# Infini-attention mix on one core: maxima turned to rows by VectorE, memory units split at head 16, first transfers in steps, later landings in the plan

## The chip, the cores and the metric

The kernel runs on one core of a Trainium2 chip. The metric is the device time of one execution in microseconds; lower is better. The core has a matrix engine (TensorE, called PE in the profile, with PEld for its weight loads), VectorE (DVE), ScalarE (ACT), GpSimd (POOL) and the queue that issues all transfers here (SyncE, SP). All five run their own instruction streams in program order and wait for each other by semaphores.

## The reference

There are two attention branches, A and B, over the same input `x` (2048 tokens, 640 features, 32 heads of 20). Each branch goes through the sequence in four segments of 512 tokens. In a segment it does causal softmax attention, reads a memory matrix that earlier segments have written, mixes both by a gate of the head, and then adds its own keys and values to the memory. A gate of the token mixes the two branches.

```python
for s in range(N):                       # four segments, in each of two branches
    logits = einsum("bhqd,bhkd->bhqk", qs, ks) * scale + mask
    a_dot = einsum("bhqk,bhkd->bhqd", softmax(logits), vs)
    num = einsum("bhld,bhde->bhle", phi(qs), M)
    den = einsum("bhld,bhd->bhl", phi(qs), z)[..., None] + 1e-6
    outs.append(g * num / den + (1.0 - g) * a_dot)
    M = M + einsum("bhld,bhle->bhde", phi(ks), vs)
    z = z + einsum("bhld->bhd", phi(ks))
out = gate * (A(x) @ A_wo) + (1 - gate) * (B(x) @ B_wo)
```

Products that need float32 precision are made of three matmuls: the high part of both operands, and each high part with the other's low part.

## The kernel before, in words

**Stages.** The work is eight windows, one for each segment and branch (segment 0 of A, segment 0 of B, segment 1 of A, and so on). A window has projections of q, k and v (`job_qk`, `job_v`: three terms of five 128-row pieces each), eight groups of four heads (a quad, numbered 0 to 63 over the run), memory reads (`mem_unit`), memory updates (`update_unit`) and an output projection (`job_o`).

**A quad** has two passes over its scores. The first (`s_unit`, L1236) computes scores with queries on the partitions, and VectorE takes the row maxima from them (L1223). The maxima, 32 numbers for each of 128 queries after a split into high and low parts (`m_unit`, L1247 on ACT and L1248 on POOL), must become rows, since they are fed back as extra rows of the operand `qst`: the second pass (`t_unit`, L1326) computes the scores with keys on the partitions, with the maximum already subtracted. ACT takes the exponential (L1318), POOL cuts the triangle (L1319), and `pv_unit` (L1346) multiplies by the values. First passes run two quads ahead of second passes, so that a quad's maxima are needed about one quad after they are made.

**Maxima to rows, before.** `mrow_unit` takes one of the eight PSUM banks and does two PE transposes (L1261, one on each half of the array). ACT then copies the bank to the tile `mr` (L1278), and two small transfers put it into `qst` (L1273).

**Two halves.** Most matmuls use 64 of the 128 rows of the array, so that two of them run side by side, one on each half (lane). The kernel fills both lanes from two lists. Projections and the other units fill the gaps between the units of the quads.

**The order is a plan.** The kernel holds a small planner that runs at build time. It keeps a clock and an assumed duration for each instruction, and it emits instructions in the order in which its own clock lets them start. `put` gives an engine an instruction, `dma` a transfer with an assumed time to land (`lat=` is added after the time that the bytes take). An engine's stream is fixed by that: where a transfer lands later than the plan assumed, the instruction that needs it stands in its engine's stream with others behind it. The table `RULES` gives, for each quad slot (the 66 steps of the main loop), the order of first-pass (S) and second-pass (T) units and seven numbers: how the slot's units are spread over its span, above which VectorE load late units are held back, the lag between the two lanes of one unit, the room kept, an earlier start and two waiting times.

**The start.** `warm_up` gives PE nine matmuls on zeros. The first two projections (q and k of the first 128 columns, `job_head`, L841) run on the whole array as the five pieces of `x` and the weights come in; nothing else can be done before. Seven more matmuls on zeros (`IDLE_STEPS`) stand among the first of them. `stage` asks for a weight piece: transfer to `wst` (three buffers), high part by ACT (L547), low part by VectorE (L549) for the first four pieces, by POOL after that. `want_x` does the same for a piece of `x` (L602, L592, L596).

**Memory reads.** `mem_unit` is called twice for each block of 128 tokens, with heads 0 to 18 and 19 to 31. The operand's channels (20 for each head) lie 128 to a tile, and each half of a tile (64 channels) is one float32 matmul, which the trace shows as two instructions. Heads that straddle a boundary of 64 channels are computed in both, with zeros where they don't belong.

Of the kernel before, what the change touches and what calls it, by code (L numbers as in the profile page):

```python
# [37 lines left out]
def r32(ap):  # L38
    return ap.bitcast(F32)
# [3 lines left out]
def tile_gated_mix_infini_attn(  # L43
# [314 lines left out]
    IDLE_STEPS = {3: 5, 4: 2}  # L358
# [136 lines left out]
    split = {}  # L495

    def stage(i):
        if i >= len(jobs) or i in staged:
            return
# [9 lines left out]
        if kind == "v":  # L509
# [6 lines left out]
            def piece(w, a, b, wh, wl, done):  # L516
# [14 lines left out]
                dma(0.53 * n, lambda: nc.sync.dma_start(out=w3, in_=src[m // 4][:, a:b, :]), landed, prio=need[i], lat=1.2)  # L531
# [4 lines left out]
        def got(w):  # L536
# [8 lines left out]
            def split_hi(pair):  # L545
                wh, wl = pair
                put("A", 0.625, lambda: nc.scalar.copy(wh, w3), lambda: put(  # L547
                    lo_eng, lo_cost,
                    lambda: lo.tensor_tensor(out=wl, in0=w3, in1=r32(wh), op=ALU.subtract), end, prio=3), prio=6)  # L549

                def end():
                    wst.give(w)
                    split[i] = pair
# [11 lines left out]
    def mix_weights(b):  # L565
# [16 lines left out]

        rows(0)

    xs = {}
    xuse = {}

    def want_x(s, k):
# [1224 lines left out]
```

## Time and profile before

| what | value |
|---|---|
| time, median of 3 runs | 1011.85 us (1010.74 to 1012.91) |
| profiled execution: its span, first to last instruction | 1010.0 us |
| the runs' median less that span | 1.85 us |
| PE busy | 998.5 us (99%) |
| VectorE busy | 751.3 us (74%) |
| ScalarE busy | 666.4 us (66%) |
| GpSimd busy | 602.4 us (60%) |
| transfers, share of 16 engines | 75.5% |

The profile gives no time of the profiled execution other than its span. A matmul's busy time holds its way through the array, in which the next one already streams, so that PE at 99% is not PE at its peak: what a matmul costs is seen from the start of one to the start of the next. Groups of instructions are named by line, engine and operation; `64*128 64x512` is a matmul on 64 rows of the array with 128 columns of weights and a 64x512 moving operand. `issue` as a releaser means that the engine waited for nothing that the profile shows.

### The profile page before, as it was taken

How to read it: one execution, taken by the hardware profiler on the slowest of the kernel's cores; microseconds unless marked ns; L12 is line 12 of the kernel's file. 1: busy time of each engine (PE TensorE's matmuls, PEld its weight loads, DVE VectorE, ACT ScalarE, POOL GpSimd, SP SyncE). 2: the span in 40 equal slices, each digit the busy share in tenths (PEclk: the TensorE clock that was granted, in tenths of full speed). 3: DMA queues.
4: the chain of work that ended last, by engine and by line, in shares of the span. 5: the costliest groups of instructions: out<-in, count | busy, mean ns of one | idle time of the engine just before them, and what ended most of it. 6: DMA issues, size and time to landing. Idle time of an engine off the chain costs nothing.

```text
span 1010.0 us, 30764 instructions
## 1 busy us (share of the span) xinstructions
PE 998.5 (99%) x11262; PEld 857.8 (85%) x11262; DVE 751.3 (74%) x2562; ACT 666.4 (66%) x1371; POOL 602.4 (60%) x1039
## 2 busy tenths in 40 slices
PE   9999999999999999999999999999999999999998
PEld 7998888978898888888889988888888897889776
DVE  4577677857897777786778857778676887789854
ACT  5476767767766677676676557766666575675682
POOL 4555657755575655666656466576675566556561
PEclk9999999999999999999999999999999999999999
DMA  7997879969796877896679677788666978658521
GB/s 241 282 313 238 284 249 317 296 197 280 241 307 211 268 224 213 255 274 204 180 227 289 196 230 229 215 273 277 200 198 201 304 235 248 201 190 269 155 89 63
DMA packets 146449, 236.42 MB, mean 234 GB/s; under 512 B 12950, under 2 KB 45883, under 8 KB 145979
## 3 DMA queue, kind: packets, MB, share of 16 engines
q1 hardware_dynamic: 146298, 234.46, 75.5%
q8 instruction: 89, 1.46, 0.6%
q14 instruction: 62, 0.50, 0.2%
HBM read 145.26 MB, written 94.65 MB: 238 GB/s over the span
## 4 chain that ended last, share of the span: by engine, by line
PE 91%; DMA 5%; DVE 2%; ACT 1%; issue 1%; SPq 0%; POOL 0%; DVEq 0%; ACTq 0%; POOLq 0%
PE bank L795 53%; PE bank L1346 14%; PE bank L1326 7%; PE bank L1236 7%; PE bank L905 3%; PE bank L987 3%; PE bank L947 2%; DMA wst<-in_a_wv_dram 1%; DMA row<-rowg 1%; PE bank L1261 1%; DMA qd<-row 1%; DMA row<-in_xT_dram 1%; DVE row L1411 1%; DMA dots<-row 1%; PE bank L1165 0%
## 5 line engine op out<-in xcount | busy, mean ns | idle before, releaser
L1223 DVE CUSTOM_DVE_ANT_0 bank<-bank,tri 128x256 f32<-128x256 f32 (+3 forms) x1024 | 474.5, 519 | 163.0 <-PE bank L1236 125.0
L795 PE MATMUL bank<-row,wh 64*128 64x512 f32 x2308 | 513.2, 402 | 0.0
L1318 ACT ACTIVATE p<-bank 128x512 f32<-128x512 f32 x548 | 301.5, 600 | 115.2 <-PE bank L1326 91.8
L795 PEld LDWEIGHTS bank<-row,wh 64*128 64x128 f32 x2308 | 329.1, 185 | 10.1 <-issue 0.2
L1319 POOL TENSOR_SCALAR_AFFINE_SELECT p<-p 128x256 f32<-128x256 f32 (+1 forms) x548 | 205.1, 382 | 200.6 <-ACT p L1318 187.1
L795 PE MATMUL bank<-row,wl 64*128 64x512 f32 x1154 | 312.5, 399 | 0.0
L549 POOL TENSOR_TENSOR wl<-wst,wh 128x640 fp32r<-128x640 f32 x115 | 180.1, 1569 | 72.7 <-ACT wh L547 69.5
L795 PE MATMUL bank<-wvh,row 64*128 64x320 f32 (+1 forms) x1280 | 191.0, 313 | 0.0
L795 PEld LDWEIGHTS bank<-row,wl 64*128 64x128 f32 x1154 | 182.9, 185 | 3.8
L1236 PE MATMUL bank<-kst,qst 60*128 60x384 f32 (+3 forms) x1024 | 177.1, 317 | 3.5 <-ACT mr L1278 2.0
L1326 PE MATMUL bank<-qst,kst 62*128 62x128 f32 (+3 forms) x1024 | 175.9, 317 | 1.3 <-DVE mx L1223 1.3
L795 PEld LDWEIGHTS bank<-wvh,row 64*128 64x128 f32 x1280 | 160.0, 185 | 2.1 <-issue 0.4
L1223 DVE DVE_READ_ACCUMULATOR2_ANT mx<- 128x1 f32 x1024 | 143.8, 140 | 0.0
L1346 PE MATMUL bank<-p,vst 128*32 128x384 f32 (+3 forms) x1836 | 141.4, 423 | 0.0
L1236 PEld LDWEIGHTS bank<-kst,qst 60*128 60x128 f32 x1024 | 132.6, 186 | 9.5 <-ACT mr L1278 2.8
L1326 PEld LDWEIGHTS bank<-qst,kst 62*128 62x128 f32 x1024 | 130.7, 186 | 6.8 <-DVE mx L1223 2.4
L1346 PEld LDWEIGHTS bank<-p,vst 128*32 128x32 f32 x1836 | 57.4, 110 | 80.9 <-issue 58.2
L795 PE MATMUL bank<-wvl,row 64*128 64x320 f32 (+1 forms) x640 | 109.1, 312 | 0.0
L547 ACT CAST wh<-wst 128x640 fp32r<-128x640 f32 x119 | 86.7, 740 | 25.1 <-PE bank L795 17.7
L795 PEld LDWEIGHTS bank<-wvl,row 64*128 64x128 f32 x640 | 87.0, 186 | 0.4 <-issue 0.2
L1376 ACT COPY row<-bank 128x512 f32<-128x512 f32 x58 | 34.2, 590 | 69.8 <-PE bank L1346 64.9
L524 POOL TENSOR_TENSOR wvl<-wst,wvh 128x640 fp32r<-128x640 f32 (+1 forms) x48 | 60.1, 1258 | 31.9 <-ACT wvh L521 30.9
(121 smaller groups left out, 1223.4 us busy)
## 6 DMA issues: line engine op xcount, KB each, us to landing
qst<-qd SPq DMA_DIRECT2D x128, 240.0 KB
kst<-kd SPq DMA_DIRECT2D x128, 240.0 KB
qd<-row SPq DMA_DIRECT2D x40, 512.0 KB
kd<-row SPq DMA_DIRECT2D x40, 512.0 KB
dots<-row SPq DMA_DIRECT2D x56, 256.0 KB
wst<-wmix SPq DMA_DIRECT2D x35, 320.0 KB
row<-dots SPq DMA_DIRECT2D x42, 256.0 KB
qd<-row SPq DMA_DIRECT2D x40, 256.0 KB
```

The source lines that it names most:

```text
L524: put("G", 0.77 * n, lambda: nc.gpsimd.tensor_tensor(out=wl[:, a:b, :VN], in0=w3, in1=r32(wh[:, a:b, :VN]), op=ALU.subtract), end, prio=4)
L547: put("A", 0.625, lambda: nc.scalar.copy(wh, w3), lambda: put(lo_eng, lo_cost, lambda: lo.tensor_tensor(out=wl, in0=w3, in1=r32(wh), op=AL ...
L549: lambda: lo.tensor_tensor(out=wl, in0=w3, in1=r32(wh), op=ALU.subtract), end, prio=3), prio=6)
L795: return nc.tensor.matmul(bank_of, lhsT=w[ROWS[half]], rhs=x_[ROWS[half]], start=start, stop=stop)
L905: return nc.tensor.matmul(pm[:, a - h0:c - h0, :].rearrange("p h e -> p (h e)"), lhsT=r32(pqTs[t, m][ROWS[half], P * n:P * (n + 1)]), rhs= ...
L1223: put("D", w / 960.0 + 0.105, lambda: nc.vector.tensor_tensor_reduce(out=sc[:, off:off + w], in0=sc[:, off:off + w], in1=tri[:, L - w:], s ...
L1236: lane_ops[half].append((mm(w), lambda pair=pair, qb=qb, off=off, w=w, r=r, sc=sc: nc.tensor.matmul(sc[:, off:off + w], lhsT=q[r, pair, P ...
L1318: put("A", 0.483, lambda: nc.scalar.activation(pt, sc, AF.Exp, scale=SCALE), lambda: (bank.give(sc), put("G", 0.15 + 0.105 * len(todo), la ...
L1319: "G", 0.15 + 0.105 * len(todo), lambda: nc.gpsimd.affine_select(out=blocks, in_=blocks, pattern=[[0, len(todo)], [1, P]], base=0, channel ...
L1326: lane_ops[half].append((mm(w), lambda pair=pair, kb=kb, off=off, w=w, r=r, sc=sc: nc.tensor.matmul(sc[:, off:off + w], lhsT=k[r, pair, P ...
L1346: nc.tensor.matmul(po[32 * j:32 * j + 32, P * kb:], lhsT=vst[t % 2][:, kb, h * E1:h * E1 + 32], rhs=pts[i, n, f][0][:, off:off + w], start ...
L1376: either(0.483, lambda: nc.scalar.copy(r32(oT), po), 0.605, lambda: nc.vector.tensor_copy(r32(oT), po), end, 2)
```

## The change

1. The maxima are turned to rows by VectorE: `mrow_unit` is gone, with its two PE transposes, its bank and its ACT copy. In its place VectorE does four transposes of 32x32 (`turn_rows`), straight from `mt` to `mr`. The two small transfers stay.
2. Memory units are split at head 16 (channel 320, a multiple of 64) and not at head 19.
3. The first transfers are issued in steps: at first three pieces of `x` are asked for, not five; the other two and the third and later weight pieces are asked for when the first piece of `x` has been split. The head's matmuls are chosen one by one as their operands' high or low parts are there, and the seven matmuls on zeros among them are gone.
4. The plan counts some transfers as landing later: v weights by 1.4 us (`lat` 1.2 to 2.6), `x` of later segments by 1.8 us, the two operands of the reciprocals by 1.0 us.
5. `RULES` has a new line for each slot.

```diff
@@ RULES
-        1: "STSTSTSTST 1.010 1.43 0.30 8 0.0 1.47 0.77",
+        1: "TTSTTSSTSS 1.01 2.38 0.3 8 0 1.6 1",
...
@@ warm_up
     WARM = 9
-    IDLE_STEPS = {3: 5, 4: 2}
@@ stage
-        if i >= len(jobs) or i in staged:
+        if i >= len(jobs) or i in staged or i >= len(HEAD0) and not x_begun:
             return
...
-                dma(0.53 * n, lambda: nc.sync.dma_start(out=w3, in_=src[m // 4][:, a:b, :]), landed, prio=need[i], lat=1.2)
+                dma(0.53 * n, lambda: nc.sync.dma_start(out=w3, in_=src[m // 4][:, a:b, :]), landed, prio=need[i], lat=2.6)
@@ want_x
             def end():
-                big.give(st)
                 xs[s, k] = (hi, lo)
+                if s:
+                    big.give(st)
+                    return
+                x_first.give(st, *([x_first_rows[-1]] if k == 0 else []))
+                if k == 0:
+                    x_begun.append(1)
+                    for i in range(len(HEAD0), 9):
+                        stage(i)
+                if k == KT - 1:
+                    big.give(*x_first_rows)
...
-                out=r32(st), in_=xT[P * k:P * (k + 1), L * s:L * (s + 1)]), landed, ..., lat=1.2 if s else 1.1)
+                out=r32(st), in_=xT[P * k:P * (k + 1), L * s:L * (s + 1)]), landed, ..., lat=3.0 if s else 1.1)
@@ job_head
-            for w, x_ in ((wh, xh), (wl, xh), (wh, xl)):
-                whole(STEP, lambda: nc.tensor.matmul(
-                    pps[i], lhsT=w[:, k, :], rhs=x_, start=(n[i] == 0), stop=(n[i] == 3 * KT - 1)))
-                n[i] += 1
-
-                for _ in range(IDLE_STEPS.get(sum(n.values()), 0)):
-                    idle_step()
-                yield STEP
+            w, o = split_hi_[i][j == 1], x_hi[0, k][j == 2]
+            whole(STEP, lambda: nc.tensor.matmul(
+                pps[i], lhsT=w[:, k, :], rhs=o, start=(n[i] == 0), stop=(n[i] == 3 * KT - 1)))
+            n[i] += 1
+            yield STEP
@@ mem_unit
-        h0, h1 = ((0, 19), (19, 32))[h]
+        h0, h1 = ((0, 16), (16, 32))[h]
@@ m_ready, mrow_unit
-        later(0, 0.2, lambda: True, lambda: mrow_unit(i))
+        mr_store.want(1, lambda mr: put("D", 0.4, lambda: turn_rows(i, mr), lambda: send_rows(i, mr), prio=1), prio=0)
+
+    def turn_rows(i, mr):
+        mt = mts.pop(i).rearrange("p f c n -> p (f c n)")
+        for j in range(NB):
+            nc.vector.transpose(r32(mr[:, 32 * j:32 * j + 32]), r32(mt[32 * j:32 * j + 32, :]))
...
-        b = bank.free.pop(0)
-        ops = [[(TURN, lambda a, z, r=r: nc.tensor.transpose(b[:32, r], mtf[r], ident[r, r]))] for r in ROWS]
...
-            put("A", 0.15, lambda: nc.scalar.copy(mr, b[:32, :P]), send, prio=1)
@@ reciprocals
-            out=r32(d), in_=lanes_of(t)[:, DH:DH + 1, :].to_broadcast([H, 4, L])), landed, prio=-1, lat=1.2)
+            out=r32(d), in_=lanes_of(t)[:, DH:DH + 1, :].to_broadcast([H, 4, L])), landed, prio=-1, lat=2.2)
...
@@ start of the program
+    big.want((F32,) * 4, lambda *rows: (x_first_rows.extend(rows), x_first.give(*rows[:3])))
     for k in range(KT):
         if k < len(HEAD0):
             stage(k)
         want_x(0, k)
-    for i in range(len(HEAD0), 9):
-        stage(i)
```

**Three places in the streams.** The first is SyncE's stream at the very start (weights to `wst`, pieces of `x` to `row`). Before:

```order
L558 DMA wst_142<-in_a_wq_dram 128x640
L602 DMA row_9_191<-in_xT_dram 128x512
L558 DMA wst_143<-in_a_wk_dram 128x640
L602 DMA row_16_194<-in_xT_dram 128x512
L602 DMA row_21_197<-in_xT_dram 128x512
L602 DMA row_26_200<-in_xT_dram 128x512
L602 DMA row_31_203<-in_xT_dram 128x512
L558 DMA wst_144<-in_a_wq_dram 128x640
L558 DMA wst_142<-in_a_wk_dram 128x640
```

and now:

```order
L566 DMA wst_142<-in_a_wq_dram 128x640
L622 DMA row_4_188<-in_xT_dram 128x512
L566 DMA wst_143<-in_a_wk_dram 128x640
L622 DMA row_5_189<-in_xT_dram 128x512
L622 DMA row_6_190<-in_xT_dram 128x512
L1746 DMA beta_199<-in_a_beta_dram 128x32
L1746 DMA beta_200<-in_b_beta_dram 128x32
L622 DMA row_4_188<-in_xT_dram 128x512
L622 DMA row_7_191<-in_xT_dram 128x512
L566 DMA wst_144<-in_a_wq_dram 128x640
```

The fourth piece of `x` goes into the buffer of the first (`row_4`), so that it and all behind it on SyncE wait until that piece has been split. The second place is PE's stream of the head (`wh`, `wl` weights; `row` the parts of `x`; `bank_134` q, `bank_135` k). Before:

```order
L349 MATMUL bank_141<-qst_80 128x512 x9
L841 MATMUL bank_134<-row_7_189,wh_145 128x512
L841 MATMUL bank_134<-row_7_189,wl_146 128x512
L841 MATMUL bank_134<-row_8_190,wh_145 128x512
L349 MATMUL bank_141<-qst_80 128x512 x5
L841 MATMUL bank_135<-row_7_189,wh_147 128x512
L349 MATMUL bank_141<-qst_80 128x512 x2
L841 MATMUL bank_135<-row_7_189,wl_148 128x512
L841 MATMUL bank_135<-row_8_190,wh_147 128x512
L841 MATMUL bank_134<-row_14_192,wh_145 128x512
```

and now:

```order
L356 MATMUL bank_141<-qst_80 128x512 x9
L868 MATMUL bank_134<-row_13_193,wh_145 128x512
L868 MATMUL bank_134<-row_13_193,wl_146 128x512
L868 MATMUL bank_134<-row_14_194,wh_145 128x512
L868 MATMUL bank_135<-row_13_193,wh_147 128x512
L868 MATMUL bank_135<-row_14_194,wh_147 128x512
L868 MATMUL bank_134<-row_20_195,wh_145 128x512
L868 MATMUL bank_135<-row_13_193,wl_148 128x512
```

The seven matmuls on zeros are gone, and the products with low parts stand behind those whose operands are there earlier. The third place is where maxima become rows. Before, on ACT, at the first v weights of the third window (`wvh` the high part of v weights, `mr` the rows, `p` exponentials):

```order
L1318 ACTIVATE p_4116_3592<-bank_138 128x512
L1318 ACTIVATE p_4117_3593<-bank_137 128x512
L521 CAST wvh<-wst_143 128x2x320
L1278 CAST mr_161<-bank_136 32x128
L1318 ACTIVATE p_4158_3623<-bank_135 128x512
L1318 ACTIVATE p_4157_3622<-bank_138 128x512
L521 CAST wvh<-wst_144 128x2x320
```

and now, on VectorE, at the same quad (`mx` the maxima of a first pass):

```order
L1247 ISA bank_139,mx_3436<-bank_139,tri 128x512
L1247 ISA mx_3436 128x1
L1283 STREAM_TRANSPOSE mr_161<-mt_3445 32x32 x4
L784 TENSOR_TENSOR row_3961_3464<-bank_136,row_3960_3463 128x512
L767 TENSOR_SCALAR bank_136<-bank_136 128x512
L768 TENSOR_TENSOR row_3962_3465<-bank_136,row_3962_3465 128x512
L1247 ISA bank_141,mx_3436<-bank_141,tri 128x384
```

The copy of the rows has left ACT, where it stood behind a cast of v weights, and the four transposes stand between two evacuations on VectorE. Counted over the streams, PE loses the 128 transposes of L1261 and 24 matmuls of `mem_unit` (264 to 240), VectorE gains 256 transposes, and ACT loses 64 copies.

More of the change, by code (lines that the diff above doesn't have):

```diff
@@ L546, in split_hi, with low @@
                 wh, wl = pair
-                put("A", 0.625, lambda: nc.scalar.copy(wh, w3), lambda: put(
-                    lo_eng, lo_cost,
-                    lambda: lo.tensor_tensor(out=wl, in0=w3, in1=r32(wh), op=ALU.subtract), end, prio=3), prio=6)
+                def low():
+                    split_hi_[i] = pair
+                    put(lo_eng, lo_cost, lambda: lo.tensor_tensor(out=wl, in0=w3, in1=r32(wh), op=ALU.subtract), end, prio=3)
+                put("A", 0.625, lambda: nc.scalar.copy(wh, w3), low, prio=6)
                 def end():
@@ L825, in job_head, with there @@
     def job_head():
-        todo = [(k, i) for k in range(KT) for i in range(len(HEAD0))]
+        todo = [(k, i, j) for k in range(KT) for i in range(len(HEAD0)) for j in range(3)]
         pps, n = {}, {}
+        def there(x):
+            k, i, j = x
+            return i in (split if j == 1 else split_hi_) and (0, k) in (xs if j == 2 else x_hi)
         while todo:
-            ready_ = [x for x in todo if x[1] in split and (0, x[0]) in xs]
-            if not ready_:
+            x = next((x for x in todo if there(x)), None)
+            if x is None:
                 blocked[0] = "head"
@@ L1253, in m_ready, with send_rows, sent @@
         m_done.add(i)
-        later(0, 0.2, lambda: True, lambda: mrow_unit(i))
-    def mrow_unit(i):
-        t, u, q, k = quad(i)
-        mt = mts.pop(i)
-        b = bank.free.pop(0)
-        mtf = r32(mt.rearrange("p f c n -> p (f c n)"))
-        ops = [[(TURN, lambda a, z, r=r: nc.tensor.transpose(b[:32, r], mtf[r], ident[r, r]))] for r in ROWS]
-        def got(mr):
-            def sent():
-                mr_done.add(i)
-                mr_store.give(mr)
-            def send():
-                bank.give(b)
-                done = then_all(2, sent)
-                for half in range(2):
-                    r = 64 * half + 60
-                    dma(0.3, lambda half=half, r=r: nc.sync.dma_start(
-                        out=r32(q[r:r + 2, :, :].rearrange("p a (b n) -> p (a b) n", b=NB)),
-                        in_=r32(mr[16 * half:16 * half + 16, :]),
-                    ), done, prio=-2, some=True, issue=0.68)
-            put("A", 0.15, lambda: nc.scalar.copy(mr, b[:32, :P]), send, prio=1)
-        return split_unit(*ops, lambda: mr_store.want(1, got))
+        mr_store.want(1, lambda mr: put("D", 0.4, lambda: turn_rows(i, mr), lambda: send_rows(i, mr), prio=1), prio=0)
[3 more added lines that the diff above has]
+            nc.vector.transpose(r32(mr[:, 32 * j:32 * j + 32]), r32(mt[32 * j:32 * j + 32, :]))
+    def send_rows(i, mr):
+        t, u, q, k = quad(i)
+        def sent():
+            mr_done.add(i)
+            mr_store.give(mr)
+        done = then_all(2, sent)
+        for half in range(2):
+            r = 64 * half + 60
+            dma(0.3, lambda half=half, r=r: nc.sync.dma_start(
+                out=r32(q[r:r + 2, :, :].rearrange("p a (b n) -> p (a b) n", b=NB)),
+                in_=r32(mr[16 * half:16 * half + 16, :]),
+            ), done, prio=-2, some=True, issue=0.68)
     def p_room():
@@ L1423, in reciprocals @@
         dma(0.8, lambda: nc.sync.dma_start(
-            out=r32(d), in_=lanes_of(t)[:, DH:DH + 1, :].to_broadcast([H, 4, L])), landed, prio=-1, lat=1.2)
+            out=r32(d), in_=lanes_of(t)[:, DH:DH + 1, :].to_broadcast([H, 4, L])), landed, prio=-1, lat=2.2)
         dma(0.8, lambda: nc.sync.dma_start(
-            out=r32(g), in_=rowg[t // 2][NB * b:NB * b + NB, :].rearrange("n p -> (n p)")[None, :].to_broadcast([P, L])), landed, prio=-1, lat=1.2)
+            out=r32(g), in_=rowg[t // 2][NB * b:NB * b + NB, :].rearrange("n p -> (n p)")[None, :].to_broadcast([P, L])), landed, prio=-1, lat=2.2)
     waiting = {}
```

21 lines of the change are left out of this document (13 added, 8 removed), and 123 rows, old and new, of the table RULES.

## The prediction

> **What bounds the kernel now.** I read the page first: the span, PE's share, then the chain that ended last, with its shares by line.
>
> ```profile
> span 1010.0 us, 30764 instructions
> PE 998.5 (99%) x11262; PEld 857.8 (85%) x11262; DVE 751.3 (74%) x2562; ACT 666.4 (66%) x1371; POOL 602.4 (60%) x1039
> PE 91%; DMA 5%; DVE 2%; ACT 1%; issue 1%; SPq 0%; POOL 0%; DVEq 0%; ACTq 0%; POOLq 0%
> by line: PE bank L795 52.8%; PE bank L1346 13.6%; PE bank L1326 7.2%; PE bank L1236 7.0%; PE bank L905 3.2%; PE bank L987 3.1%; PE bank L947 2.2%; DMA wst<-in_a_wv_dram 1.4%; DMA row<-rowg 0.9%; PE bank L1261 0.9%; DMA qd<-row 0.9%; issue 0
> ```
>
> PE is busy for 99% of the span and is 91% of the chain. Work that leaves PE's stream is therefore worth its step in that stream, and work on another engine is worth something only where PE waits for it. How often PE waits is said by the waits of PE alone:
>
> ```profile
> PE bank L1236 <- ACT mr L1278: 2.0, 2, 1.5
> PE bank L349 <- DVE qst L353: 1.5, 1, 1.5
> PE bank L1326 <- DVE mx L1223: 1.3, 1, 1.3
> PE bank L1236 <- ACT p L1318: 0.9, 2, 0.7
> PE bank L1236 <- ACT vst L1042: 0.6, 1, 0.6
> PE bank L947 <- DVE row L751: 0.4, 1, 0.4
> ```
>
> Without the start (L349) and the head (L947) that is 2.0 + 1.3 + 0.9 + 0.6 = 4.8 us in the whole run. The largest wait is for the ACT copy that the change removes. The timeline of PE and ACT around it shows why:
>
> ```profile
> 217.29 0.39 PE L1236 MATMUL bank<-kst,qst 60*128 60x512 f32 x1
> 219.13 0.50 PE L1236 MATMUL bank<-kst,qst 60*128 60x512 f32 x1 [1.45 <-ACT mr L1278]
> 218.20 0.72 ACT L521 CAST wvh<-wst 128x640 fp32r<-128x640 f32 x1 [2.16 <-DMA wst<-in_a_wv_dram]
> 218.83 0.25 ACT L1278 CAST mr<-bank 32x128 fp32r<-32x128 f32 x1
> ```
>
> ACT stands 2.16 us before a cast whose transfer has not landed; behind it stands the copy of the rows, which holds a bank, and PE waits 1.45 us for that bank.
>
> **The change part by part.** First, what leaves PE. From the groups of instructions, with shapes apart where it matters:
>
> ```profile
> L1261 PE MATMUL bank<-ident,mt 64*32 64x64 f32 x128 | 28.1, 219 | 0.2
> L1261 PEld LDWEIGHTS bank<-ident,mt 64*32 64x32 f32 x128 | 11.9, 93 | 9.1 <-issue 7.3 <-POOL row L1319 0.4 <-PE bank L795 0.3
> L947 PE MATMUL bank<-ident,row 64*128 64x64 f32 x304 | 31.5, 226 | 0.4 <-DVE row L751 0.4
> L947 PE MATMUL bank<-ident,O 64*128 64x64 f32 x240 | 19.5, 227 | 0.1
> L905 PE MATMUL bank<-mbd,row 64*128 64x84 f32 x432 | 47.8, 274 | 0.0
> L905 PE MATMUL bank<-mbd,row 64*128 64x63 f32 x48 | 8.5, 264 | 0.0
> L905 PE MATMUL bank<-mbd,row 64*128 64x21 f32 x48 | 8.1, 247 | 0.0
> ```
>
> The means of 219 to 274 ns hold the way through the array, so the steps come from the chain. The transposes of maxima have 0.9% of 1010.0 us, 9.1 us or 71 ns each for 128. The like transposes of L947 have 2.2%, 22.2 us for 304 + 240 = 544, 41 ns each; at that price 128 are 5.2 us. Weight loads before L1261 also stand 7.3 us idle, a part of which other half-array work covers. Bounds 0 (they fill holes beside the other half) and 9.1 us; I take **6.5 us**, nearer the like transposes.
>
> Memory units lose the pieces with 21 columns (head 19 alone), 48 instructions; 48 others grow from 63 to 84 columns. L905 has 3.2%, 32.3 us for 528, 61 ns each: 2.9 us go. Growing costs 274 - 264 = 10 ns for each of 48, 0.5 us, at most. **2.5 us**, bounds 0 and 2.9. On VectorE the two weighings change from 19 and 13 heads to 16 and 16, the same in sum.
>
> Second, what VectorE takes on: 256 transposes of 32x32, which this trace does not show. The nearest rows are small operations:
>
> ```profile
> L1223 DVE DVE_READ_ACCUMULATOR2_ANT mx<- 128x1 f32 x1024 | 143.8, 140 | 0.0
> L919 DVE SCALAR_TENSOR_TENSOR mw<-bank,gq 128x19 f32<-128x19 f32 x24 | 4.1, 171 | 1.6 <-PE bank L905 1.6
> L921 DVE RECIPROCAL mw<-mw 128x19 f32<-128x19 f32 x24 | 6.6, 276 | 0.8
> 275.00:400.00 125.00, 125.00 (x1443) 109.05 (x1440) 100.10 (x327) 82.42 (x168) 78.70 (x135) 1.00 0.80 245
> DVE bank L1223 <- PE bank L1236: 125.0, 141, 7.5
> ```
>
> Between 140 and 276 ns each, 256 make 35.8 to 70.7 us; I take 171 ns, 43.8 us, 0.68 us for a quad. VectorE then has 751.3 + 43.8 = 795 us. In its busiest stretch, the row 275:400 (VectorE is the third busy time), it has 100.1 of 125 us; eight quads more make 105.6, at the upper price 108.9. It stays under the bound, and its pauses before the maxima (125.0 us, 141 times, 0.89 us each) cover 0.68 us. I cost it at **0 us**; without that cover it is the second rival below. The ACT copies that go (64 of 249 ns, 15.9 us) are worth only the 2.0 us of PE's wait for them. The rows now pass from POOL to VectorE to the transfers, one engine less, and the second passes that wait for them come a quad later.
>
> Third, **the waits**. The change takes away the bank and the copy behind 2.0 of the 4.8 us. The transfers counted as later bear on that wait and on the 1.3 us one, which comes from the reciprocals:
>
> ```profile
> 418.12 0.75 DVE L1406 SCALAR_TENSOR_TENSOR row<-row,gcol,row 128x512 f32<-128x512 f32 x1 [2.62 <-DMA row<-rowg]
> 668.29 0.62 ACT L592 CAST row<-row 128x512 fp32r<-128x512 f32 x1 [3.12 <-DMA row<-in_xT_dram]
> ```
>
> VectorE stood 2.62 us before L1406 and ACT 3.12 us before a piece of `x`, each with other work behind. Counting 1.0 and 1.8 us more moves such instructions back, but by less than these waits. I take all of the 2.0, half of the other 2.8, and give back 0.4 for new waits of the new order: **3.0 us**. Bounds: 4.8 gained, and 4.8 lost if the new order has twice the waits. The table itself has no row; I price it at nothing beyond that, with 4 us either way, the size of all present waits.
>
> Fourth, **the head**. The timeline of PE, VectorE and ACT at the start:
>
> ```profile
> 1.52 4.21 PE L349 MATMUL bank<-qst 128*128 128x512 f32 x9 [1.52 <-DVE qst L353]
> 5.52 0.78 PE L841 MATMUL bank<-row,wh 128*128 128x512 f32 x1
> 6.69 1.31 PE L349 MATMUL bank<-qst 128*128 128x512 f32 x5
> 14.70 0.39 PE L841 MATMUL bank<-row,wh 128*128 128x512 f32 x1
> 15.02 0.27 PE L642 MATMUL bank<-ident,row 64*128 64x64 f32 x1
> 5.49 0.69 DVE L596 TENSOR_TENSOR row<-row,row 128x512 fp32r<-128x512 f32 x1
> 8.95 2.77 DVE L596 TENSOR_TENSOR row<-row,row 128x512 fp32r<-128x512 f32 x4 [1.58 <-ACT row L592]
> 3.83 0.73 ACT L547 CAST wh<-wst 128x640 fp32r<-128x640 f32 x1 [1.74 <-DMA wst<-in_a_wq_dram]
> 8.29 2.70 ACT L592 CAST row<-row 128x512 fp32r<-128x512 f32 x4 [1.78 <-DMA row<-in_xT_dram]
> 0.81 0.39 SPq L558 DMA_DIRECT2D wst<-in_a_wq_dram  x1
> ```
>
> The head's 30 matmuls lie between 5.52 and 15.02, 9.5 us. Next to each other they start about 0.235 us apart (five in 1.31 us, of which the last ends 0.39 after it starts: 0.92 / 4 = 0.23), 7.0 us for 30. So at most 2.5 us are to be had. Four pieces of `x` land together at 8.29, since four were asked for at once; now two are, and with half as much asked for they should land about 1 us earlier (an estimate). The last two are asked for after the first piece is split, at 5.49 + 0.69 = 6.2; a lone transfer here took 0.81 to 3.83, 3.0 us, so they land near 9.5 and 10, and with a cast of 0.7 and a subtraction of 0.7 the last is ready at 11.5, as before (8.95 + 2.77 = 11.7). PE then is bound by its own 24 matmuls from about 7.6: 13.2, and with small pauses 13.5. I take **1.5 us**; bounds 2.5 gained and 1.9 lost (the fourth rival).
>
> The first nine matmuls take 4.21 / 9 = 0.47 us each, and the five on zeros start 0.23 apart; the page of the Trainium skill "TensorE: Matmul & The Clock Gate", Part 1, says that the array starts at half clock, gets the full one after about 3.4 us of activity and loses it after an idle window as long. The trace agrees with the first half of that; by the second half the fillers can go as long as no pause lasts 3.4 us, and the sum stays as it is.
>
> **Sum**, against the profiled span: 1010.0 - 6.5 - 2.5 - 3.0 - 1.5 = 996.5 us. The runs' median lay 1011.85 - 1010.0 = 1.85 us over the span: **998.4 us**.
>
> **The rivals.** *PE's holes take it.* If transposes and short pieces lay where the other half was streaming, taking them away gives nothing, and 1010.0 - 3.0 - 1.5 + 1.85 = 1007.4 us. For it: PE's halves are filled from two lists. Against it: the chain gives L1261 71 ns each, more than its like. Chance 0.10.
>
> *VectorE holds PE.* The four transposes wait for POOL's subtraction L1248, and POOL's stream has long work:
>
> ```profile
> L549 POOL TENSOR_TENSOR wl<-wst,wh 128x640 fp32r<-128x640 f32 x115 | 180.1, 1569 | 72.7 <-ACT wh L547 69.5 <-DVE mx L1223 1.8 <-PE bank L1236 0.4
> DVE bank L1223 <- POOL mt L1248: 2.4, 1, 2.4
> ```
>
> If L1248 falls behind one of these, VectorE stands up to 1.57 us and then works 0.68, with the evacuations of the first passes behind it and PE short of banks. Of 2.25 us the mean pause covers 0.89; 1.36 us in one quad of four is 16 x 1.36 = 22 us: 998.4 + 22 = 1020 us. It decides once PE loses over 13.5 / 64 = 0.21 us in a quad. Against it: such meetings must come often, and now VectorE's maxima meet a late L1248 once, for 2.4 us. Chance 0.06.
>
> *New waits.* The new table and the later landings change where transfers and engines meet. Three times the 4.8 us, 14.4, instead of 1.8 that I leave, make 998.4 + 12.6 = 1011.0 us. For it: each of the present waits is an accident of one order. Against it: the counts go toward what the trace shows. Chance 0.09, of which 0.06 no change, 0.02 slower, 0.01 faster.
>
> *A slow head.* If PE without its fillers stays at the start's 0.47 us for eight matmuls more, 8 x 0.24 = 1.9 us are lost where 1.5 were gained: 998.4 + 1.5 + 1.9 = 1001.8 us. Against it stands that its pauses will be short. The clock gate above is this mechanism. Chance 0.05. That the change does less than it says, I leave out: the streams show transposes, pieces and transfers where it puts them.
>
> **How the numbers follow.** The forecast has 0.70, the rivals 0.10, 0.06, 0.09 and 0.05. About 2 us (0.2%) can be told from no change. Faster: 0.70 + 0.10 + 0.05 + 0.01 = 0.86; the same 0.06; slower 0.06 + 0.02 = 0.08. The best case is 9.1 + 2.9 + 4.8 + 2.5 = 19.3 us and 4 for the order: 988.6. For eight times in ten I cut that to 990 and take the holes rival in: 990 to 1008.
>
> **What would show it.** Right: no L1261; some 43 us more on VectorE in 256 transposes of about 0.17 us; 480 instructions in place of 528 for memory units; a head that ends near 13.5; PE's waits for engines under 4 us. Wrong: PE waiting for VectorE's maxima or for banks in many quads; transposes well over 0.3 us; PE's shares of all other lines grown by as much as the two lines lost.

## The result, and the profile after

| | median, us | lowest to highest | profiled span, us |
|---|---|---|---|
| before | 1011.45 (4 runs) | 1010.74 to 1012.91 | 1010.0 |
| changed | 998.3 (4 runs) | 997.94 to 999.33 | 996.5 |

The ratio of the changed kernel to the one before is 0.9878, with a 95% interval of 0.9859 to 0.9896: faster by 1.2%. Both the time and the span (996.5 us) came out where the prediction put them. The sections below show that several of its terms did not.

The head of the changed kernel's page has its span, the busy time of the engines, and the shares of the chain that ended last:

```profile
span 996.5 us, 30494 instructions
PE 989.4 (99%) x11079; PEld 843.6 (85%) x11079; DVE 794.0 (80%) x2818; ACT 654.1 (66%) x1305; POOL 603.4 (61%) x1041
PE 98%; DMA 1%; DVE 0%; SPq 0%; issue 0%; ACT 0%
```

PE still sets the time, and holds 98% of the chain, where it had 91%. The pieces of the chain that led over transfers (5%) are almost gone. The waits of PE alone, which had six rows before, have two:

```profile
PE bank L356 <- DVE qst L360: 1.5, 1, 1.5
PE bank L868 <- ACT row L602: 0.4, 2, 0.2
```

Both belong to the start. Of the 4.8 us of waits in the body none is left. The groups that replace L1261 and the split at head 19, and what VectorE waits for most (total, times, longest):

```profile
L1283 DVE STREAM_TRANSPOSE mr<-mt 32x32 f32<-32x32 f32 x256 | 51.0, 199 | 26.5 <-POOL mt L1272 23.9
L929 PE MATMUL bank<-mbd,row 64*128 64x84 f32 x480 | 46.5, 273 | 0.0
DVE bank L1247 <- PE bank L1260: 95.2, 126, 4.8
DVE mr L1283 <- POOL mt L1272: 23.9, 28, 2.4
```

A transpose takes 199 ns. The pauses before the maxima are 95.2 / 126 = 0.76 us each now, against 0.89. In 28 of the 64 quads VectorE stands before its transposes until POOL has the split maxima ready, 23.9 us in all. The timeline of VectorE shows the four transposes of one quad, and the table of stretches (PE, PEld, VectorE, ACT and POOL busy, with their counts) the stretch in which VectorE is now busiest and the one that the prediction spoke of:

```profile
103.90 0.84 DVE L1283 STREAM_TRANSPOSE mr<-mt 32x32 f32<-32x32 f32 x4
775.00:900.00 125.00, 125.00 (x1419) 106.95 (x1417) 105.30 (x362) 80.27 (x158) 74.97 (x129) 1.00 0.81 245
275.00:400.00 125.00, 124.94 (x1412) 106.50 (x1411) 103.45 (x362) 82.08 (x161) 79.16 (x135) 1.00 0.82 248
```

The four take 0.84 us, more than a pause of 0.76 us. The plan counts 0.4 us for them.

**Where the time went** can be read from the starts of the matmuls. The next table adds up, in each of the two traces, the time from the start of each PE instruction to the start of the next one, by the line of the first of the two. The last instruction counts with its own length. With 1.5 us ahead of the first and some 4 to 5 us behind the last, these steps make up the span.

| instructions | before: count, us | after: count, us | difference, us |
|---|---|---|---|
| projections (L795, L818) | 5400, 555.2 | 5400, 551.8 | -3.4 |
| transposes of maxima (L1261) | 128, 3.5 | none | -3.5 |
| first passes (L1236, L1260) | 1024, 89.0 | 1024, 86.8 | -2.2 |
| memory reads (L905, L929) | 528, 35.5 | 480, 33.3 | -2.3 |
| memory updates (L987, L1011) | 480, 36.9 | 480, 35.0 | -1.9 |
| matmuls on zeros (L349, L356) | 16, 5.6 | 9, 4.4 | -1.2 |
| the rest | 3686, 278.2 | 3686, 278.8 | +0.6 |

These are 14.0 us less in steps (before rounding), with 0.5 us more behind the last matmul. The table compares one execution with one. The traces of experiments 1 and 7 below have the order of the kernel before, and show how far executions of that order differ: 552.8 and 552.6 us for the projections, 87.6 and 87.7 us for the first passes, 36.0 and 35.6 for the memory reads, 36.6 and 38.6 for the updates. So most of the 3.4 us of the projections and of the 2.2 us of the first passes lies within that scatter, while memory reads and updates are shorter in the changed kernel than in all three. Such a table says where the steps are shorter, and not why.

### The profile page after: what moved, and what is told of

It is laid out like the page before. It is cut to its first block, busy times and chain, and to the rows that moved or that the text cites. A ratio compares the mean times of both kernels' runs of the same rounds, so it can differ in the third digit from the quotient of the medians.

```text
span 996.5 us, 30494 instructions
## 1 busy us (share of the span) xinstructions
PE 989.4 (99%) x11079; PEld 843.6 (85%) x11079; DVE 794.0 (80%) x2818; ACT 654.1 (66%) x1305; POOL 603.4 (61%) x1041
## 3 DMA queue, kind: packets, MB, share of 16 engines
q8 instruction: 87, 1.43, 0.6%
## 4 chain that ended last, share of the span: by engine, by line
PE 98%; DMA 1%; DVE 0%; SPq 0%; issue 0%; ACT 0%
PE bank L818 58%; PE bank L1364 15%; PE bank L1344 8%; PE bank L1260 8%; PE bank L1011 3%; PE bank L929 3%; PE bank L971 3%; PE bank L868 1%; DMA row<-in_xT_dram 1%; PE bank L1189 0%; DVE row L1174 0%; SPq L566 0%; ACT row L602 0%; PE bank L701 0%; DVE gate L643 0%
## 5 line engine op out<-in xcount | busy, mean ns | idle before, releaser
L1247 DVE CUSTOM_DVE_ANT_0 bank<-bank,tri 128x128 f32<-128x128 f32 (+3 forms) x1024 | 474.4, 520 | 104.0 <-PE bank L1260 95.2
L818 PE MATMUL bank<-row,wh 64*128 64x512 f32 x2308 | 497.2, 402 | 0.0
L1336 ACT ACTIVATE p<-bank 128x512 f32<-128x512 f32 x562 | 308.1, 603 | 122.1 <-PE bank L1344 104.7
L818 PEld LDWEIGHTS bank<-row,wh 64*128 64x128 f32 x2308 | 320.8, 185 | 13.0 <-issue 1.4
L818 PE MATMUL bank<-row,wl 64*128 64x512 f32 x1154 | 295.4, 398 | 0.0
L818 PE MATMUL bank<-wvh,row 64*128 64x320 f32 (+1 forms) x1280 | 183.3, 313 | 0.0
L818 PEld LDWEIGHTS bank<-row,wl 64*128 64x128 f32 x1154 | 175.5, 185 | 6.1 <-issue 1.2
L1344 PE MATMUL bank<-qst,kst 62*128 62x512 f32 (+3 forms) x1024 | 174.2, 321 | 0.0
L1260 PE MATMUL bank<-kst,qst 60*128 60x384 f32 (+3 forms) x1024 | 171.5, 316 | 0.1
L818 PEld LDWEIGHTS bank<-wvh,row 64*128 64x128 f32 x1280 | 153.1, 185 | 1.9 <-issue 0.8
L1260 PEld LDWEIGHTS bank<-kst,qst 60*128 60x128 f32 x1024 | 128.5, 186 | 7.9 <-issue 1.5
L818 PE MATMUL bank<-wvl,row 64*128 64x320 f32 (+1 forms) x640 | 107.8, 311 | 0.0
L818 PEld LDWEIGHTS bank<-wvl,row 64*128 64x128 f32 x640 | 87.1, 185 | 0.6 <-issue 0.2
L1283 DVE STREAM_TRANSPOSE mr<-mt 32x32 f32<-32x32 f32 x256 | 51.0, 199 | 26.5 <-POOL mt L1272 23.9
```

The source lines that it names most:

```text
L818: return nc.tensor.matmul(bank_of, lhsT=w[ROWS[half]], rhs=x_[ROWS[half]], start=start, stop=stop)
L1247: put("D", w / 960.0 + 0.105, lambda: nc.vector.tensor_tensor_reduce(out=sc[:, off:off + w], in0=sc[:, off:off + w], in1=tri[:, L - w:], s ...
L1260: lane_ops[half].append((mm(w), lambda pair=pair, qb=qb, off=off, w=w, r=r, sc=sc: nc.tensor.matmul(sc[:, off:off + w], lhsT=q[r, pair, P ...
L1283: nc.vector.transpose(r32(mr[:, 32 * j:32 * j + 32]), r32(mt[32 * j:32 * j + 32, :]))
L1336: put("A", 0.483, lambda: nc.scalar.activation(pt, sc, AF.Exp, scale=SCALE), lambda: (bank.give(sc), put("G", 0.15 + 0.105 * len(todo), la ...
L1344: lane_ops[half].append((mm(w), lambda pair=pair, kb=kb, off=off, w=w, r=r, sc=sc: nc.tensor.matmul(sc[:, off:off + w], lhsT=k[r, pair, P ...
```

## The experiments

The twelve kernels were measured in three groups of four, each group on another chip, and the kernel before was measured anew beside each group. Each time is set against the median before of its own group: 1011.13 us for doubled transposes on PE, maxima back on PE, doubled transposes on VectorE and the plan with 0.36 us; 1010.43 for half the transposes, the swap, the short pieces and the matmuls on zeros; 1010.3 for the other four. The changed kernel stood 13.15 us under its own.

**1. What do the PE transposes cost?** In the kernel before, each is issued twice, at the same place.

```diff
-        ops = [[(TURN, lambda a, z, r=r: nc.tensor.transpose(b[:32, r], mtf[r], ident[r, r]))] for r in ROWS]
+        ops = [[(TURN, lambda a, z, r=r: [nc.tensor.transpose(b[:32, r], mtf[r], ident[r, r]) for _ in range(2)][-1])] for r in ROWS]
```

> The kernel before, with each of its 128 PE transposes of maxima issued twice in place, so that 128 more stand in the same stream and nothing else moves; the output is the same. My step (they stand in PE's path at 41 to 71 ns each): 5.2 to 9.1 us more than before, about 6.5. The rival that they fill holes beside the other half of the array: within 1.5 us of before.

Measured: 1014.43 us (12 runs), ratio 1.0034, interval 1.002 to 1.0048. That is 3.3 us for 128 more transposes (2.0 to 4.9), 26 ns each (16 to 38). The steps in the table above say 3.5 / 128 = 27 ns. In this run's own trace the 256 transposes have 8.7 us of steps, 5.2 us more than the 128 before, 41 ns for each added one, so that 26 ns is no exact price. By the times this term is about 3.4 us and at most 4.9, not the 6.5 us that I took. Why the chain's share of 0.9% says more is not shown. What PE would gain without its transposes, and with nothing in their place, was not run. The Trainium skill, page "TensorE: Matmul & The Clock Gate", Part 1 (in the section on 56 ns and 53.3 ns), gives the time from start to start as the number of columns over 2.4 GHz, and 2.5 ns. For 64 columns that makes 29 ns, an estimate that lies within the 16 to 38 ns of the runs; it would have given 3.7 us.

**2. The maxima back on PE in the changed kernel**, everything else as changed: `mrow_unit`, bank and ACT copy instead of `turn_rows`.

```diff
-        mr_store.want(1, lambda mr: put("D", 0.4, lambda: turn_rows(i, mr), lambda: send_rows(i, mr), prio=1), prio=0)
+        later(0, 0.2, lambda: True, lambda: mrow_unit(i))
```

> The changed kernel with the maxima turned to rows by PE and copied by ACT, as before; all else as changed. The plan makes a new order of it. My steps: 6.5 us for the transposes and up to 2.0 us for a wait behind the copy, 1004.8 to 1006.8 us. If PE's holes take the transposes: under 1001 us. If VectorE's new work had cost PE time, this kernel would be faster than 998 us.

Measured: 1049.21 us, ratio 1.0371 (1.0348 to 1.0395). It does not price the step: with other durations the planner emits another order everywhere.

**3. Other orders.** How much the order alone weighs, three kernels show: the changed one with 0.36 us in place of 0.4 planned for the four transposes (the work is the same), the changed one with the table of before, and the kernel before with the new table.

```diff
-        mr_store.want(1, lambda mr: put("D", 0.4, lambda: turn_rows(i, mr), ...
+        mr_store.want(1, lambda mr: put("D", 0.36, lambda: turn_rows(i, mr), ...
```

> The changed kernel with the planned cost of the four transposes on VectorE 0.36 us in place of 0.4, which changes no work but makes the plan put instructions in another order. It measures what a new order alone is worth. If single steps can be told from orders: within 2 us of 998.3. If orders are worth as much as the steps: 3 to 8 us off, to the slower side, since the table was made for the other order.

> The changed kernel with the table of the kernel before. If the new table only adjusts (my 4 us either way): 994 to 1003 us. If a table fits one plan alone, as the run with another planned cost says (70 us slower by a plan cost of 0.36 for 0.4): 1030 to 1080 us.

> The kernel before with the new table. If the new table is better in itself: under 1011 us. If a table fits one plan alone: 1030 to 1080 us.

Measured: 1068.25 us, ratio 1.0562 (1.0539 to 1.0585); 1071.69 us, ratio 1.0604 (1.0582 to 1.0627); and 1061.95 us, ratio 1.0508 (1.0484 to 1.0531). A planned duration that differs by 0.04 us costs 70 us against the changed kernel; the table of the other kernel costs 73 us there and 52 us in the kernel before. So in these cases a table fits its own plan alone, and undoing one edit of the changed kernel measures the new order, not the edit. From here on I used only kernels that keep an order instruction for instruction.

Where does a bad order lose? In part by the clock. In the kernel with 0.36 us the mean granted clock is 0.984 of 1066.4 us, so about 1066.4 x 0.016 = 17 us of clock are missing (an estimate). Six stretches of 2 us of it, with the same columns as above (the one before the last two figures is the granted clock), and PE's timeline there:

```profile
178.00:180.00 2.00, 1.41 (x7) 0.67 (x5) 1.63 (x2) 1.97 (x5) 2.00 (x4) 1.00 0.64 219
180.00:182.00 2.00, 1.33 (x7) 0.86 (x7) 2.00 (x6) 2.00 (x5) 2.00 (x3) 0.96 0.07 24
182.00:184.00 2.00, 2.00 (x15) 2.00 (x14) 2.00 (x11) 1.81 (x4) 2.00 (x3) 0.50 0.00 0
184.00:186.00 2.00, 2.00 (x15) 2.00 (x14) 1.65 (x12) 0.00 (x0) 2.00 (x4) 0.50 0.14 38
186.00:188.00 2.00, 2.00 (x17) 2.00 (x15) 0.64 (x2) 0.00 (x0) 2.00 (x3) 0.50 0.42 126
188.00:190.00 2.00, 2.00 (x20) 1.90 (x19) 1.41 (x4) 0.82 (x2) 0.84 (x3) 0.84 0.00 0
178.68 0.43 PE L1260 MATMUL bank<-kst,qst 60*128 60x384 f32 x1 [0.19 <-ACT p L1336]
179.51 0.50 PE L1260 MATMUL bank<-kst,qst 60*128 60x384 f32 x3 [0.40 <-ACT vst L1066]
181.62 5.86 PE L1011 MATMUL bank<-vst,row 64*128 64x168 f32 x35 [0.64 <-ACT p L1336]
```

PE is busy for 1.41 and 1.33 of 2 us, with no pause over 0.64 us; then the clock stands at a half for 6.8 us (and in three later stretches, 34.1 us in all), and 35 memory updates take 5.86 us, 167 ns each, where the changed kernel's table above has 35.0 / 480 = 73 ns. The other 53 us or so of the loss lie spread over the stream; I did not trace them to single waits.

**4. Is VectorE's new work free?** The changed kernel's order is kept, and each transpose is issued twice, or only two of the four are issued, or none.

```diff
-        for j in range(NB):
+        for j in [j for j in range(NB) for _ in range(2)]:
             nc.vector.transpose(r32(mr[:, 32 * j:32 * j + 32]), r32(mt[32 * j:32 * j + 32, :]))
```

> The changed kernel with each of the 256 VectorE transposes issued twice in place; the order and the output are the same. VectorE gets some 51 us more work by the profile (256 of 199 ns). My step (VectorE's pauses cover it): within 1.5 us of the changed kernel's 998.3. The rival that VectorE holds PE: 0.2 us and more in each of 64 quads, over 1010 us.

> The changed kernel with two of each four VectorE transposes left out (half of the maxima are zeros then, set once at the start); the order is kept. VectorE has some 25 us less. My step (VectorE's pauses cover the transposes): within 1.5 us of 998.3. The rival that VectorE holds PE already: at the price of the doubled transposes (27 us for 51) up to 13 us faster, 985 to 995.

> The changed kernel with all four VectorE transposes of each quad left out (all maxima in the second passes are zeros, set once at the start); the order is kept. It prices VectorE's part in the changed kernel in full. By the half that was left out (4.7 us faster for 25 us less): if VectorE's first microseconds are the dearest, 5 to 7 us faster than 998.3 in all; if the price is even, 9.4 us faster, 989. My step in the prediction (nothing) would be 998.3 and fell already with the half.

| transposes for a quad | time, us | ratio to before (interval) | against before, us |
|---|---|---|---|
| none | 993.71 | 0.983 (0.981 to 0.985) | -16.6 |
| two | 993.62 | 0.9836 (0.9824 to 0.9849) | -16.8 |
| four (the change) | 998.3 | 0.9878 (0.9859 to 0.9896) | -13.15 |
| eight | 1025.14 | 1.0137 (1.0116 to 1.0159) | +14.0 |

Two are free. Four cost 4.6 us as the medians stand, 3.4 us when each is set against its own before; the profiled spans, 992.1 and 996.5, say 4.4. Eight cost 27 us more than four. The price is nothing up to a point and then bends upward. It is not the standing before POOL that costs: with two transposes VectorE still stands 24.0 us for it, in 28 quads as with four, and the kernel is as fast as without any.

```profile
DVE mr L1283 <- POOL mt L1272: 24.0, 28, 2.4
```

With eight, PE's waits and those of its weight loads name VectorE's maxima:

```profile
PE bank L1344 <- DVE mx L1247: 3.3, 6, 0.9
PE bank L1260 <- DVE mx L1247: 2.7, 6, 0.7
PE bank L971 <- DVE row L774: 2.6, 4, 0.9
PEld bank L1344 <- DVE mx L1247: 7.7, 16, 1.2
PE 73%; DVE 14%; DMA 4%; issue 3%; POOL 2%; ACT 2%; SPq 1%; POOLq 0%; DVEq 0%; ACTq 0%
```

VectorE has 14% of the chain there. With four, no row of the matmuls' waits names VectorE behind the start, and yet 4 us are lost. The waits of the weight loads do name its maxima, in short pieces. The largest row with four:

```profile
PEld bank L1344 <- DVE mx L1247: 2.1, 9, 0.3
```

With none this row has 1.0 us in 5 times. All weight loads together wait for the maxima 15 times and 3.3 us with four, 7 times and 1.6 us with none (1.4 us with two). The steps of the projections (worked out as in the table above) are 548.1 us with none and 548.6 with two, where the changed kernel has 551.8: 3.7 of the 4.4 us in the spans lie there. How the waits of the weight loads become these longer steps I did not follow one by one.

**5. The swap by itself.** The kernel before, with its own order. The PE transposes and the ACT copy are taken out of it, and the four transposes of VectorE are put in where the copy was planned, and VectorE's stream has no planned room for them. The bank is still taken.

```diff
-        ops = [[(TURN, lambda a, z, r=r: nc.tensor.transpose(b[:32, r], mtf[r], ident[r, r]))] for r in ROWS]
+        ops = [[(TURN, lambda a, z: None)] for r in ROWS]
...
-            put("A", 0.15, lambda: nc.scalar.copy(mr, b[:32, :P]), send, prio=1)
+            put("A", 0.15, lambda: [nc.vector.transpose(r32(mr[:, 32 * j:32 * j + 32]), mtf[32 * j:32 * j + 32, :]) for j in range(NB)], send, prio=1)
```

> The kernel before, its order and plan kept: the 128 PE transposes and the 64 ACT copies of maxima are left out, and the four VectorE transposes stand where the ACT copy was called for, though the plan does not know of them. The output is the same. My steps (PE's path shorter by the transposes, the 2.0 us wait for the ACT copy gone, VectorE's work free): 3.4 (by the run with doubled transposes) to 6.5 and 2.0, so 1002.5 to 1006 us. The rival from the doubled VectorE transposes (51 us of unplanned VectorE work cost 27 us): 1025 to 1035 us, slower than before.

Measured: 1032.12 us, ratio 1.0212 (1.0198 to 1.0226): 21.7 us slower than before, though PE does 128 transposes less. Its page and its waits:

```profile
PE 1011.0 (98%) x11134; PEld 850.7 (83%) x11134; DVE 798.1 (77%) x2818; ACT 657.4 (64%) x1307; POOL 602.5 (58%) x1039
PE bank L1236 <- DVE mx L1223: 3.9, 10, 0.7
PE bank L1326 <- DVE mx L1223: 1.7, 5, 0.6
PEld bank L1236 <- DVE mx L1223: 10.6, 18, 0.9
```

VectorE is at 77% of the span and its evacuations are late all the same: its order is fixed, and 0.83 us for each quad that no plan has room for push all that stands behind it. Here too it is not the standing before POOL: VectorE stood for POOL's maxima in 3 quads only, 2.5 us in all. In this order the swap loses; it pays, if at all, together with an order made for it.

**6. Do the short pieces of the memory reads cost anything?** The kernel before, its order kept, without the 48 instructions of 21 columns (so that a part of head 19's read is left out).

```diff
+            if c - a == 1:
+                carry[half] = start
+                return None
```

> The kernel before with the 24 memory matmuls of 21 columns (head 19's first four channels) left out, and the order of all else kept; head 19's memory read lacks these channels. My step (61 ns for each of 48 instructions): 2.9 us faster, about 1008.5. If they fill holes beside the other half: within 1 us of before.

Measured: 1010.99 us (12 runs), ratio 1.0006 (0.9994 to 1.0018). That is no gain: the interval runs from 0.6 us faster to 1.8 us slower, and 2.9 us lie outside it. The steps of its trace say little here. The remaining 480 have 36.1 us, where all 528 had 35.5, but in this one execution the clock stood at a half from 458.2 us on for 6.8 us, and 23 of the 480 took 3.64 us in that stretch, 158 ns each where the like ones take 66. Without it the 480 would have some 34 us (an estimate), 1.5 us less than the 528; the 48 short pieces alone have 3.4 us of steps before. That they stood in holes which stay when they go fits the times, and is not shown by the steps.

**7. Does PE need the matmuls on zeros in the head?** The kernel before without the seven.

```diff
-    IDLE_STEPS = {3: 5, 4: 2}
+    IDLE_STEPS = {}
```

> The kernel before without the seven matmuls on zeros in the head; the order of all else is kept and the output is the same. My step (PE waits for pieces of x there anyway): 0 to 1 us faster. The rival of a slow head (the array stays at the spacing of the start): 1.9 us slower or more, and the head's matmuls 0.4 us apart after 8 us.

Measured: 1012.42 us (12 runs), ratio 1.0011 (0.9997 to 1.0026): no change that can be told. Its timeline of PE, from its fastest run:

```profile
7.72 0.50 PE L841 MATMUL bank<-row,wl 128*128 128x512 f32 x1 [0.30 <-DVE wl L549]
8.06 0.62 PE L841 MATMUL bank<-row,wh 128*128 128x512 f32 x2
8.52 0.40 PE L841 MATMUL bank<-row,wl 128*128 128x512 f32 x1
8.76 0.63 PE L841 MATMUL bank<-row,wh 128*128 128x512 f32 x2
13.98 0.27 PE L642 MATMUL bank<-ident,row 64*128 64x64 f32 x1
```

From 8.06 on the matmuls start 0.23 us apart (8.06 to 8.52 for two, 8.52 to 8.76 for one), as they did with the fillers. The head ends at 13.98 in place of 15.02, yet the median, 2.0 us above the one before, does not show the microsecond: it is lost again further on in this order, or too small beside the spread (1009.4 to 1014.5).

**8. A cheaper transpose?** The changed kernel, its compute order kept, with two transposes of 64 partitions in place of four of 32. The rows then lie on two groups of partitions, so that four transfers for a quad replace two.

```diff
-        for j in range(NB):
-            nc.vector.transpose(r32(mr[:, 32 * j:32 * j + 32]), r32(mt[32 * j:32 * j + 32, :]))
+        for j in range(2):
+            nc.vector.transpose(r32(mr[:, 32 * j:32 * j + 32]), r32(mt[64 * j:64 * j + 64, :]))
```

> The changed kernel with two transposes of 64 partitions for each quad in place of four of 32, and four transfers of 64 short runs in place of two (half the tokens of a row in each); the plan is not told and the order is kept, the output is the same. If VectorE's time is what holds PE: up to 4.7 us faster than 998.3, about 994. If the 128 more transfers on SyncE (some 0.4 to 0.7 us each to issue) delay others: no change or slower.

Measured: 1003.0 us (6 runs), ratio 0.9932 (0.991 to 0.9954): still faster than before, but 4.7 us slower than the change (5.9 when each is set against its own before). The group of transposes, PE's waits and the chain:

```profile
L1287 DVE STREAM_TRANSPOSE mr<-mt 64x32 f32<-64x32 f32 x128 | 26.0, 203 | 24.1 <-POOL mt L1276 23.1
PE bank L1264 <- DMA kst<-kd: 3.0, 2, 1.7
PE bank L1264 <- ACT row L989: 1.4, 1, 1.4
PE 90%; DMA 6%; DVE 1%; ACT 1%; SPq 1%; issue 1%; POOL 0%; ACTq 0%; DVEq 0%; POOLq 0%
```

VectorE's work is halved (26.0 for 51.0 us), which alone was worth 3.4 to 4.6 us above. The two more transfers for a quad take more than that back: PE now waits 3.0 us for `kst`, and transfers are again 6% of the chain. No kernel tried with the whole computation beats the changed one.

## Why the prediction was right or wrong

The total was right: 998.4 us were forecast and 998.3 measured. The direction and the main line of the mechanism, a shorter stream on PE with fewer waits in it, were right too. That the total met to 0.1 us is luck: nearly all of its terms were off in size, the largest part of the gain came from what I had put at nothing, and the errors cancelled.

- **PE's transposes**: mis-sized. 6.5 us predicted, 3.3 (2.0 to 4.9) measured by doubling them. The failing step was to lay their price between the like transposes and the chain's share. The chain gave these 71 ns and the like ones 41; the steps from start to start give these 27, and the like ones 27.7 / 544 = 51. The chain is no price list for single small matmuls.
- **Memory units**: 2.5 us predicted, nothing measured when the short pieces alone go. The 2.3 us that the table of steps shows for this group in the changed kernel are no scatter (the traces of the old order have 35.5 to 36.0 us, the changed one 33.3), but experiment 6 does not give them to the short pieces; I put them down to the new order. The first rival, that PE's holes take it, fits this term and not the transposes.
- **VectorE at nothing**: wrong in size, right in kind. 199 ns were measured for the 171 I took; a quad's four take 0.84 us, for 0.68. My cover was a pause of 0.89 us; the pauses are 0.76 now. Two transposes are indeed covered, four cost 3.4 to 4.6 us. The mean of the pauses did not cover each quad. That VectorE would have 795 us in all, and 105.6 us in the stretch 275:400, was nearly met (794.0 and 103.45), and said nothing of this.
- **The waits**: 3.0 us predicted; all of the 4.8 us are gone, the upper bound. In the traces of experiments 1, 6 and 7, which have the order of before, such waits sum to 4.1, 5.2 and 3.0 us, so the 4.8 is good to a microsecond or two.
- **The head**: 1.5 us predicted, 0.9 measured (it ends at 14.14 for 15.02). The second pieces of `x` landed about 1 us earlier, as estimated, with ACT's cast of them at 7.29 for 8.29:

```profile
7.97 0.50 PE L868 MATMUL bank<-row,wh 128*128 128x512 f32 x1 [0.19 <-ACT row L602]
14.14 0.50 PE L818 MATMUL bank<-row,wh 64*128 64x512 f32 x1
7.29 1.25 ACT L602 CAST row<-row 128x512 fp32r<-128x512 f32 x2 [0.45 <-DMA row<-in_xT_dram]
10.49 1.12 ACT L602 CAST row<-row 128x512 fp32r<-128x512 f32 x2
```

  The start of PE's matmuls slipped from 5.52 to 5.91, and ACT cast the last two pieces from 10.49, so that they were ready at 12.4, about a microsecond later than the 11.5 I had. Whether the 0.9 us reach the end is not shown; in experiment 7 about as much did not.
- **The table at nothing**: this failed most. The parts that I can read off singly are gains of 3.3, 4.8 and 0.9 us and a loss of 3.4 to 4.6, about 5 us of the 13.5 in the spans. The other 8 or 9 us (an estimate) are left to the new order as a whole. The table of steps has some 2 us of it each in the memory reads and the updates; the 3.4 us of the projections are in large part scatter. My bound of 4 us either way, from the size of PE's waits, was too narrow on both sides: in experiment 3 other orders lie 52 to 61 us above the kernel before.

Of the rivals, *VectorE holds PE* was real, though not by the mechanism that I gave it. I let VectorE stand for POOL in one quad of four; it stands in 28 of 64, 23.9 us in all, and experiment 4 shows that this alone costs nothing. What costs is VectorE's own added work, 27 us with eight transposes and 21.7 us in the old order. It did not decide here since the new order leaves room for most of the 0.84 us, though its plan counts only 0.4. *New waits* did not come. *A slow head* fell: the trace of the changed kernel has the full pace from 8.30 on, and experiment 7 from 8.06.

What stays open: how the 8 or 9 us of the order divide between the later landings, the table, and the bank that `mrow_unit` no longer takes. Each of them changes the plan, and experiment 3 shows that a changed plan under an unchanged table says nothing of the part. Undoing the later landings or the steps of the first transfers alone was not tried for that reason. Nor was another table for the kernel before, fitted to its own plan: a part of the 8 or 9 us may be to be had without the change.

## What to carry to other kernels

In a kernel whose order is written by a planner, an edit and its re-planned order are one change: price an edit with the order kept, by doubling or leaving out its instructions in place, and expect the order itself to weigh more than most edits. Work moved to an engine at 74% was free here up to half of it, and its price bent upward beyond that. The waits of PE's matmuls showed none of it at first; those of its weight loads did, so both are to be read. A total that comes out right does not vouch for its terms: one of these was out by a factor of two, and one was worth nothing.

## What the runs showed of the hardware that was not expected

- **The clock falls without a long pause.** In the kernel with 0.36 us the granted clock went to a half at about 181.8 us, after some 4 us in which PE was busy for 67 to 70% and never paused longer than 0.64 us, and came back after 6.8 us. The Trainium skill, page "TensorE: Matmul & The Clock Gate", section "HAM oscillation — how this bites in real kernels", states as the rule that pauses of PE should not pass about 3.4 us. Here the trace differs: the clock fell though every pause was far shorter, so that keeping to the rule is not enough. The busy share of PE does not decide it alone either: in the trace of experiment 8 PE was busy for 1.98 of 3.41 us (439.13 to 442.54) and paused for 1.43 us, and the clock stayed full. What decides is not shown. In the profiles of the two kernels of the case the clock stays full behind the start; in the one of experiment 6, with the order of before, it fell for 6.8 us behind a pause of 1.82 us.
- **Small transposes on VectorE** take 199 ns for 32x32 in float32, and 203 ns for 64x32, in which each block of 32 partitions is transposed in its own place. So in these two sizes the price is for the instruction, not for the partitions, and 64 at a time cost half as much.
- **A matmul of 64 columns** on half of the array cost 26 ns (16 to 38) where it was added to PE's full stream, though its duration in the profile is 219 ns.
